# Mixture of experts behind an attention: the last remainders of w2, the token gathers and one part's weight sums in other places

## The chip, the core and the metric

The kernel runs on one core of a Trainium2 chip. The metric is the device time of one execution in microseconds (us); a run is one execution, and the times of several runs are given by their median. The engines are TensorE (PE in the profile; PEld is its weight load), VectorE (DVE), ScalarE (ACT), GpSimd (POOL) and SyncE (SP, which issues transfers). Each engine works through its own queue in order.

## What is computed

An attention over 8 batches and 8 heads (576 rows, 64 columns each, with a decay and a causal mask) gives 4608 tokens of 512 values. A gate picks one of 8 experts for each token, and the expert's two weight matrices are applied to its tokens:

```python
def _moe_ref(x, w_gate, w1, w2):          # x: 4608 x 512, w1: 8 x 512 x 1024, w2: 8 x 1024 x 512
    logits = x @ w_gate
    expert_idx = np.argmax(logits, axis=1)
    ...
    for e in range(E):
        mask = expert_idx == e
        ...
        xe = x[mask]
        h = np.maximum(xe @ w1[e], 0.0)
        ye = h @ w2[e]
        out[mask] = gate_w[mask, None] * ye
    return out.astype(np.float32)
```

## The kernel before

The attention comes first, then the experts one after the other. Expert 0 has a form of its own; the change concerns the experts 1 to 7, which the loop at L1677 runs. Each has room for 640 tokens, in five blocks of 128. Values are kept as two words, a rounded one and a remainder, so that a product is made of three matmuls: rounded by rounded, remainder by rounded, rounded by remainder.

**The ups** (h = relu(x w1)) are 28 steps, k = 0 to 27: four groups (`group`) of seven products each (`product`, L1513, six matmuls a step), a scheme that gets by with seven products of half blocks where eight would be needed. Part i of w1 belongs to group i. A matmul has 320, 288 or 256 columns, by the expert's count of tokens (`by_count`, which branches on PE). Between the products, `after(s)` puts together the four results of a group in banks a, b, g, d: ACT copies p1 = a at s = 0 and p5 = g at s = 2 (L1575, which frees bank g for step 6 of the group); at s = 5 DVE adds b to p1 (L1579), takes it off d (L1580), and POOL adds p1 to p5 (L1581). The rest stands in the next group's first steps: ACT's relu of d and of p5 (L1559, into the rounded h, `hhw`) and of g, DVE's L1590, and DVE's remainders `rest` (L1562, into `hl`). The fourth group's are handed on to the downs as `self.ends`. For group 0 of expert 1 the relu of p5 stands a step later, behind that of g (`late`), and p5 lies in a tile y.

**The downs** (h w2) take a block of 128 tokens each (`down`, m = 0 to 4): 24 matmuls of 512 columns (L1275), eight slices ft of h by three terms, in the order ft = 0, 1, 2, 4, 5, 6, 3, 7. Block 0 (`head`) leaves its last terms to `finish_down`, which comes behind the first six matmuls of block 1. The last block is left out where the expert has no tokens for it, as in expert 5. ACT scales each block (L1303), and POOL scatters it to the output (L1306).

**What runs beside it** is hung on step numbers by hand: `at(ups, (k, f))` puts f behind step k of the ups, `at(dns, ...)` behind a quarter of a block of the downs. `S(...)` is work for this expert, `N(...)` for the next. For w1: `load_s` (SP, L1390), `sums_s` (POOL, four adds L1396 to L1399, tile w1r), `round_s` (ACT, L1411, w1s) and `rest_s` (DVE, or POOL where G is named, L1417); `split_s` is the last two. For w2, in four parts of two slices ft each: `load_v` (SP), `round_v` (ACT, L1456, tile w_0w or w_1w ahead of the remainder) and `rest_v` (DVE, L1449, its remainder); `split_v` is both. For the next expert's tokens: `fetch` (POOL, an indirect gather from x_dram, L1156, tile xg), `put` and `get` (SP, out and back in another layout), `flip` (DVE, L1178).

Of the kernel before, what the change touches and what calls it, by code (L numbers as in the profile page):

```python
# [22 lines left out]
S = 576  # L23
# [15 lines left out]
FT = FF // P  # L39
# [135 lines left out]
def psum(pool):  # L175
    return pool.tile([P, 512], F32, name="ps", tag="ps")
# [13 lines left out]
def attention_all(c, tc, qkT, va, vb, f, wgd, x_dram, batch_done, more_consts, extra):  # L190
# [659 lines left out]
    def run(f):  # L850
        step(f)
        order.pin()

    return run, todo


# [216 lines left out]
class Moe:  # L1073
# [185 lines left out]
    def down(self, e, m, part=(0, FT)):  # L1259

        c, nc = self.c, self.nc
        rows = self.rows_of_h(e, m)
        if part[0] == 0:
            self.py[m] = psum((c.ps_v, c.ps_m)[m % 2])
        py = self.py[m]
        terms = [(ft, *i) for ft in ((0, 1, 2, 4, 5, 6, 3, 7) if e else range(FT))
                 for i in ((0, 0), (0, 1), (1, 0))]
        tail, head = (e > 0 and m == t for t in (NST - 1, 0))
        if head:
            terms.sort(key=lambda t: t in ((6, 0, 1), (7, 0, 1)))  # L1270

        def some(k0, k1):
            for k in range(k0, k1):
                ft, hi_, wi = terms[k]
                c.note(nc.tensor.matmul(  # L1275
                    py, rows(hi_, ft), self.w2p[e, ft][wi],
                    start=k == 0, stop=k == len(terms) - 1, skip_group_check=tail or head,
                ))

        if tail:  # L1280
            some(0, 1)
            few = self.tail
            if e + 1 < E:
                self.begin_up(e + 1)
            else:
                self.tc.mark_branch_hint_location("overflow", engines=[mybir.EngineType.PE])
            with self.tc.If(few > 0):  # L1287
                some(1, len(terms))
        else:
            some(3 * part[0], 3 * part[1] - (2 if head and part[1] == FT else 0))  # L1290
        if part[1] < FT:
            return
        if head:
            self.finish_down = lambda: (some(len(terms) - 2, len(terms)), self.down_out(e, m, py, tail))
        else:
            self.down_out(e, m, py, tail)

# [326 lines left out]
    def run(self, run, tasks):  # L1624
        c, tc = self.c, self.tc
        T = lambda f, *args: lambda: f(*args)
        fetch = lambda e, m: T(self.fetch, e, m)
        self.s, self.parts, self.slots = {}, {}, 0

        def downs(e, ms, tasks):  # L1630
            k = 0
            for m in ms:
                for q in range(4):
                    if e and m == NST - 1:
                        if q == 0:
                            run(lambda: self.down(e, m))
                    else:
                        run(lambda: self.down(e, m, (2 * q, 2 * q + 2)))
                        if e and (m, q) == (1, 0):
                            run(self.finish_down)  # L1640
                    for f in tasks.get(k, []):
                        run(f)
                    k += 1

        with tc.tile_pool(name="moe_w2b", bufs=1, side="right") as w2b:
            self.w2pools.append(w2b)
            self.finish(run, tasks)
            c.note = lambda r: r
            run(lambda: self.begin_h(0, 1))
            S = lambda f, *args: T(f, 1, *args)  # L1650
            self.load_s(1, 0)
            first = {
                0: [S(self.begin_t), fetch(1, 2), fetch(1, 0)],
                2: [S(self.sums_s, 0)], 3: [S(self.turn_t, 3), fetch(1, 1)],
                4: [S(self.turn_t, 4)], 5: [S(self.turn_t, 2)], 6: [S(self.split_s, 0, 0)],
                7: [S(self.turn_t, 0)],
            }
            for ft in range(FT):
                run(lambda: self.up(0, 1, ft))
                for f in first.get(ft, []):  # L1660
                    run(f)
            run(S(self.load_s, 1))
            downs(0, (NA, NA + 1), {
                0: [S(self.turn_t, 1), S(self.split_s, 0, 1), S(self.load_s, 2)],
                1: [S(self.split_t, "T2"), S(self.split_t, "T1")],
                2: [S(self.sums_s, 1), S(self.split_t, "T4"), S(self.split_t, "T3")],
                4: [S(self.split_s, 1, 0), S(self.sums_s, 2)],
                5: [S(self.split_s, 1, 1), S(self.load_s, 3)],
            })
        self.w2st.close()  # L1670
        with tc.tile_pool(name="moe_h", bufs=1) as hp, tc.tile_pool(name="moe_u", bufs=1) as up_, \
                tc.tile_pool(name="moe_r", bufs=2) as self.wr:
            self.up_ = up_
            hl = hp.tile([P, FT * CAP], F32R, name="hl")
            h = [t.rearrange("p (f s) -> p f s", s=CAP) for t in (c.words["hh"], hl)]
            G = self.nc.gpsimd
            for e in range(1, E):  # L1677
                self.h[e] = h
                if e == 1:
                    run(lambda: self.begin_up(e))  # L1680
                S = lambda f, *args: T(f, e, *args)
                N = lambda f, *args: T(f, e + 1, *args)
                ups, dns = {}, {}

                def at(d, *items):
                    for k, f in items:
                        d.setdefault(k, []).append(f)

                late = 9 if e == 1 else 1
                at(ups, (0, S(self.load_v, 0)), (0, S(self.load_v, 1)),  # L1690
                   (4, S(self.round_s, 2, 1)), (6, S(self.rest_s, 2, 1, G)),
                   (late, S(self.load_v, 2)), (late, S(self.load_v, 3)),
                   (9 if e > 1 else 8, S(self.split_s, 3, 0)), (11, S(self.round_s, 3, 1)),
                   (13, S(self.rest_s, 3, 1, G)))
                for i, k in enumerate((15, 22, 16) if e == 1 else (10, 23, 16)):
                    at(ups, (k, S(self.split_v, i)))
                at(ups, (23 if e == 1 else 24, S(self.round_v, 3)))
                if e == 1:
                    at(ups, (0, S(self.sums_s, 3)), (2, S(self.split_s, 2, 0)))
                else:  # L1700
                    at(ups, (8, self.scatter))
                if e + 1 < E:
                    at(ups, (9, N(self.load_s, 0)), (16, N(self.load_s, 1)),
                       (6, fetch(e + 1, 3)), (6, fetch(e + 1, 4)), (13, fetch(e + 1, 2)),
                       (15, fetch(e + 1, 0)), (19, fetch(e + 1, 1)), (20, N(self.sums_s, 0)),
                       (27, N(self.sums_s, 1)))
                    for m, i, k in ((3, 12, 16), (4, 13, 17), (2, 18, 22), (0, 21, 26), (1, 25, 27)):
                        at(ups, (i, N(self.put, m)), (k, N(self.get, m)))
                    at(dns, (0, N(self.begin_t)), (1, N(self.round_s, 0, 0)),
                       (1, N(self.round_s, 0, 1)), (2, N(self.flip, 3)), (2, N(self.flip, 4)),  # L1710
                       (2, N(self.turn_t, 3)), (2, N(self.turn_t, 4)),
                       (2, N(self.rest_s, 0, 0, G)), (2, N(self.rest_s, 0, 1, G)),
                       (6, N(self.flip, 2)), (6, N(self.flip, 0)), (6, N(self.turn_t, 2)),
                       (7, N(self.turn_t, 0)), (7, N(self.load_s, 2)),
                       (7, N(self.split_s, 1, 0)), (8, N(self.round_s, 1, 1)),
                       (8, N(self.rest_s, 1, 1, G)), (8, N(self.flip, 1)),
                       (10, N(self.turn_t, 1)), (11, N(self.load_s, 3)),
                       (12, N(self.split_t, "T2")), (12, N(self.split_t, "T1")),
                       (12, N(self.sums_s, 2)), (14, N(self.split_t, "T4")),
                       (14, N(self.split_t, "T3")), (15, N(self.split_s, 2, 0)),  # L1720
                       (15, N(self.sums_s, 3)))
                else:
                    at(ups, (27, lambda: tc.keep_in_program_order(G.drain())))
                self.ends = [lambda: None] * 3
                self.sevens(e, run, ups)
                dns.setdefault(0, [])[:0] = [*self.ends, T(self.rest_v, 3)]
                downs(e, range(NST), dns)


# [224 lines left out]
```

## Time and profile before

| | |
|---|---|
| median of 3 runs | 727.88 us (727.53 to 728.06) |
| the profiled execution's own time | 727.32 us |
| its span | 725.5 us |
| granted clock of PE | 0.994 |
| busy share of the span: PE, DVE, ACT, POOL | 99%, 77%, 69%, 79% |
| matmuls | 6321 |

Matmuls overlap, and the ends that the trace gives for them are modelled. So a pause of PE is read from the distance between the starts of two matmuls, against the distance that they have where nothing is in the way. A number in square brackets behind a row is idle time of the engine ahead of it, with the instruction that ended it; where PE's records overlap, the number there is smaller than the pause between starts.

### The profile page before, as it was taken

Reading aid. Unit: us, or ns where it says so; the run is one execution under the profiler, and the core shown is the slowest. Engines: PE = TensorE matmul, PEld = TensorE weight load, DVE = VectorE, ACT = ScalarE, POOL = GpSimd, SP = SyncE. Lnnn points to the kernel's source line nnn. Section 1 sums busy time; section 2 is a strip of 40 time slices with the busy share of each in tenths; the row PEclk is TensorE's granted clock in tenths of the full one; section 3 lists DMA queues with packets and bytes.
Section 4 is the critical chain, followed back from the end, with each engine's and each line's share of the span. In section 5 each row is a group of like instructions: output and inputs, shape, how many; then the busy total and the mean of one; then the engine's idle time right before and its main releaser. Section 6 shows DMA issues by size and latency. Waiting matters only on the chain. (4 is left out here: it accounts for less than half of the span.)

```text
span 725.5 us, 18440 instructions
## 1 busy us (share of the span) xinstructions
PE 715.7 (99%) x6321; PEld 617.2 (85%) x6321; DVE 555.9 (77%) x1608; ACT 497.9 (69%) x1319; POOL 573.7 (79%) x702
## 2 busy tenths in 40 slices
PE   9999999999999999999999999999999999999997
PEld 4788888888888888798999898898898888988985
DVE  6668888888888888861879959779589599897730
ACT  6999999999999999562646555566465566655631
POOL 6999989898898898965589779778788797997511
PEclk9999999999999999999999999999999999999999
DMA  6775787766776767334349476386475574673300
GB/s 199 196 193 163 195 215 194 205 197 204 207 205 191 222 187 233 118 117 125 114 150 269 132 231 206 109 249 196 144 208 171 198 214 147 215 208 101 141 30 35
DMA packets 98724, 127.59 MB, mean 176 GB/s; under 512 B 10287, under 2 KB 56367, under 8 KB 98608
## 3 DMA queue, kind: packets, MB, share of 16 engines
q1 hardware_dynamic: 91568, 106.12, 50.3%
q0 software_dynamic: 6400, 19.93, 8.6%
q8 instruction: 71, 1.16, 0.7%
q14 instruction: 45, 0.37, 0.2%
q10 hardware_dynamic: 640, 0.01, 0.0%
HBM read 99.12 MB, written 27.93 MB: 175 GB/s over the span
## 5 line engine op out<-in xcount | busy, mean ns | idle before, releaser
L422 ACT ACTIVATE sc<-sc,nmx 128x512 f32<-128x512 f32 (+3 forms) x256 | 142.4, 558 | 5.3 <-DVE nmx L379 4.2
L1513 PE MATMUL ps<-X_0w,w1s 128*128 128x320 f32 (+2 forms) x504 | 107.0, 303 | 0.7 <-ACT u L1575 0.4
L1275 PE MATMUL ps<-w_0w,hl 128*128 128x512 f32 x272 | 107.3, 395 | 0.0
L1275 PE MATMUL ps<-w_0w,hhw 128*128 128x512 f32 x273 | 106.4, 390 | 0.6 <-ACT hhw L1559 0.6
L1275 PE MATMUL ps<-w_1w,hhw 128*128 128x512 f32 x272 | 105.5, 392 | 0.0
L1306 POOL DMA_INDIRECT out<-y,si_fast x40 | 48.1, 1202 | 59.5 <-ACT y L1303 27.9
L467 ACT COPY aT<-ps 128x512 f32<-128x512 f32 (+1 forms) x224 | 93.4, 507 | 1.8 <-PE ps L455 0.5
L330 POOL TENSOR_TENSOR hl<-raw,hl 128x640 fp32r<-128x640 f32 (+1 forms) x60 | 89.5, 1492 | 5.0
L526 PE MATMUL ps<-aT,va_t 128*64 128x256 f32 (+3 forms) x896 | 91.0, 354 | 0.0
L1513 PEld LDWEIGHTS ps<-X_0w,w1s 128*128 128x128 f32 x504 | 82.3, 188 | 1.2 <-ACT u L1575 0.7
L526 PEld LDWEIGHTS ps<-aT,va_t 128*64 128x64 f32 x896 | 56.6, 137 | 29.0 <-issue 5.3
L403 PE MATMUL ps<-hl 64*128 64x512 f32 (+1 forms) x720 | 80.7, 340 | 0.0
L1513 PE MATMUL ps<-X_1w,w1s 128*128 128x320 f32 (+2 forms) x252 | 75.9, 301 | 0.0
L1303 ACT ACTIVATE y<-ps,g_fast 128x512 f32<-128x512 f32 x40 | 28.0, 699 | 59.5 <-PE ps L1275 51.4
L379 DVE CUSTOM_DVE_ANT_0 sc<-ps,bias 128x128 f32<-128x128 f32 (+1 forms) x128 | 59.8, 486 | 9.3 <-PE ps L403 4.6
L1417 POOL TENSOR_TENSOR w1s<-w1r,w1s 128x768 fp32r<-128x768 f32 (+1 forms) x32 | 62.8, 1968 | 0.1
L1275 PEld LDWEIGHTS ps<-w_0w,hhw 128*128 128x128 f32 x273 | 51.3, 188 | 12.4 <-ACT hhw L1559 1.4
L1275 PEld LDWEIGHTS ps<-w_1w,hhw 128*128 128x128 f32 x272 | 51.1, 188 | 11.5
L1275 PEld LDWEIGHTS ps<-w_0w,hl 128*128 128x128 f32 x272 | 51.1, 188 | 11.1 <-DVE hl L1562 0.6
L379 DVE CUSTOM_DVE_ANT_1 sc<-ps,bias 128x256 f32<-128x256 f32 (+1 forms) x128 | 57.7, 487 | 3.0 <-POOL gT L709 1.7
L1513 PE MATMUL ps<-xa,w1s 128*128 128x320 f32 (+2 forms) x336 | 56.0, 302 | 0.3 <-PEq L1287 0.3
L403 PEld LDWEIGHTS ps<-hl 64*128 64x128 f32 x720 | 52.6, 185 | 3.3
(251 smaller groups left out, 1895.4 us busy)
## 6 DMA issues: line engine op xcount, KB each, us to landing
bias<-ud SPq DMA_DIRECT2D x30, 576.0 KB, 5.8
w1r<-in_w SPq DMA_DIRECT2D x112, 128.0 KB, 2.6
w<-in_w SPq DMA_DIRECT2D x28, 512.0 KB, 5.7
raw<-in_qkT SPq DMA_DIRECT2D x64, 160.0 KB, 3.5
raw<-in_qkT SPq DMA_DIRECT2D x64, 144.0 KB, 3.4
va_t<-in_va SPq DMA_DIRECT2D x32, 256.0 KB, 5.8
x_dram<-row SPq DMA_DIRECT2D x32, 256.0 KB, 2.4
xs<-xg SPq DMA_DIRECT2D x30, 256.0 KB, 3.9
```

Source lines behind the costliest of these rows:

```text
L330: return eng.tensor_tensor(hl[:, 1], raws[n][:, r : r + w], hl[:, 0].bitcast(F32), ALU.subtract)
L379: red_last[:] = [V.tensor_tensor_reduce(dst, src, in1, -0.125, init, ALU.add, ALU.min, nms[n][:, col : col + 1]).ins]
L403: note(nc.tensor.matmul(pb[j][:, o : o + w], q[js], k[js], start=(i == 0), stop=(i == len(terms) - 1),))
L422: A.activation(x, x, AF.Exp, bias=nms[n][:, 5 * j + t : 5 * j + t + 1], scale=-1.0, accum_out=ssums[b][:, t, 2 * p + j : 2 * p + j + 1])
L467: copy_on = {"a": lambda o, i: A.copy(o, i), "v": lambda o, i: V.tensor_copy(o, i)}
L526: note(nc.tensor.matmul(pv[j * HD : (j + 1) * HD, q0 - qa : qb - qa], l, r, start=(blk == 0), stop=(blk == nb - 1),))
L1275: c.note(nc.tensor.matmul(py, rows(hi_, ft), self.w2p[e, ft][wi], start=k == 0, stop=k == len(terms) - 1, skip_group_check=tail or head,))
L1303: nc.scalar.activation(y, py, AF.Copy, scale=g[:, s : s + 1])
L1306: nc.gpsimd.indirect_dma_start(out=self.out, out_offset=bass.IndirectOffsetOnAxis(ap=si[:, s : s + 1], axis=0), in_=y, in_offset=None, bou ...
L1417: (eng or self.nc.vector).tensor_tensor(lo, raw, hi.bitcast(F32), ALU.subtract)
L1513: self.nc.tensor.matmul(bank[:, 0:cols], w[:, wi, mat, kt], x[xi][:, kt, 0:cols], start=start and k == 0, stop=k == 5, skip_group_check=True,)
```

## The change

1. **w2.** In block 0 of the downs of the experts 1 to 7, four terms are left to `finish_down` instead of two: those with the remainder of w2's slices 2, 3, 6 and 7, which are the parts 1 and 3. So 20 matmuls come first, then six of block 1, then four. The remainder of part 1 (`rest_v(1)`) moves from step 23 (22 in expert 1) of the ups to the start of the downs, ahead of that of part 3 and behind what is left of the fourth group.
2. **Gathers.** In the experts 2 to 6 the gathers for the next expert stand behind the steps 1, 1, 8, 8 and 13 instead of 6, 6, 13, 15 and 19; puts and gets go with them, and the load of the next expert's part 1 of w1 goes from step 16 to 20.
3. **Expert 1's sums.** `sums_s(3)` goes from step 0 to step 5, where it stands behind `after(5)` of group 0, and the rounding and remainder of its first half from step 8 to 10.

No engine gets more or fewer instructions.

```diff
         if head:
-            terms.sort(key=lambda t: t in ((6, 0, 1), (7, 0, 1)))
+            late = [(ft, 0, 1) for ft in (2, 3, 6, 7)]
+            terms.sort(key=lambda t: t in late)
...
-            some(3 * part[0], 3 * part[1] - (2 if head and part[1] == FT else 0))
+            n = len(terms) - len(late) if head else 3 * FT
+            some(min(3 * part[0], n), min(3 * part[1], n))
...
-            self.finish_down = lambda: (some(len(terms) - 2, len(terms)), self.down_out(e, m, py, tail))
+            self.finish_down = lambda: (some(n, len(terms)), self.down_out(e, m, py, tail))
...
-                   (9 if e > 1 else 8, S(self.split_s, 3, 0)), (11, S(self.round_s, 3, 1)),
+                   (9 if e > 1 else 10, S(self.split_s, 3, 0)), (11, S(self.round_s, 3, 1)),
...
-                for i, k in enumerate((15, 22, 16) if e == 1 else (10, 23, 16)):
+                for i, k in ((0, 15), (2, 16)) if e == 1 else ((0, 10), (2, 16)):
                     at(ups, (k, S(self.split_v, i)))
-                at(ups, (23 if e == 1 else 24, S(self.round_v, 3)))
+                for i, k in ((1, 22), (3, 23)) if e == 1 else ((1, 23), (3, 24)):
+                    at(ups, (k, S(self.round_v, i)))
                 if e == 1:
-                    at(ups, (0, S(self.sums_s, 3)), (2, S(self.split_s, 2, 0)))
+                    at(ups, (2, S(self.split_s, 2, 0)), (5, S(self.sums_s, 3)))
...
-                    at(ups, (9, N(self.load_s, 0)), (16, N(self.load_s, 1)),
-                       (6, fetch(e + 1, 3)), (6, fetch(e + 1, 4)), (13, fetch(e + 1, 2)),
-                       (15, fetch(e + 1, 0)), (19, fetch(e + 1, 1)), (20, N(self.sums_s, 0)),
-                       (27, N(self.sums_s, 1)))
-                    for m, i, k in ((3, 12, 16), (4, 13, 17), (2, 18, 22), (0, 21, 26), (1, 25, 27)):
+                    if e == 1:
+                        gathers = (6, 3), (6, 4), (13, 2), (15, 0), (19, 1)
+                        ways = (3, 12, 16), (4, 13, 17), (2, 18, 22), (0, 21, 26), (1, 25, 27)
+                    else:
+                        gathers = (1, 3), (1, 4), (8, 2), (8, 0), (13, 1)
+                        ways = (3, 11, 15), (4, 12, 16), (2, 17, 21), (0, 19, 23), (1, 26, 27)
...
-                dns.setdefault(0, [])[:0] = [*self.ends, T(self.rest_v, 3)]
+                dns.setdefault(0, [])[:0] = [
+                    *self.ends, T(self.rest_v, 1), T(self.rest_v, 3)]
```

On POOL, the first steps of expert 6 before (as in the experts 2 to 5): the last sum of a part of w1, the add to p5 of group 0 (u_104), a remainder of w1, then two gathers, a scatter, and the add of group 1.

```order
L1399 TENSOR_TENSOR w1r<-w1r 128x256
L1525 UNCONDITIONAL_BRANCH
L1581 TENSOR_TENSOR u_104<-u_96,u_104 128x320
L1417 TENSOR_TENSOR w1s<-w1r,w1s 128x768
L1156 DMA xg<-x_dram,gi_fast 128x512 x2
L1306 DMA out<-y,si_fast 4608x512
```

The same place after (the lines have moved on by two):

```order
L1401 TENSOR_TENSOR w1r<-w1r 128x256
L1156 DMA xg<-x_dram,gi_fast 128x512 x2
L1527 UNCONDITIONAL_BRANCH
L1583 TENSOR_TENSOR u_104<-u_96,u_104 128x320
L1419 TENSOR_TENSOR w1s<-w1r,w1s 128x768
L1308 DMA out<-y,si_fast 4608x512
L1156 DMA xg<-x_dram,gi_fast 128x512 x2
```

The first pair of gathers now stands ahead of the add of group 0, and the second pair ahead of that of group 1.

On DVE, the end of an expert's fourth group before: a remainder of w2 (into w_0_1w, part 1) stands ahead of the add to p1, and that of part 3 (w_1_1w) behind the last `rest`.

```order
L1449 TENSOR_TENSOR w_0_1w<-w_0_1_94,w_0_0w 128x1024
L1579 TENSOR_TENSOR u_13567<-ps,u_13567 128x320
L1580 TENSOR_TENSOR pr<-u_13567,pr 128x320
L1562 SCALAR_TENSOR_TENSOR hl<-ps,hhw 128x320
L1590 TENSOR_TENSOR ps<-ps,u_13708 128x320
L1562 SCALAR_TENSOR_TENSOR hl<-pr,hhw 128x320
L1562 SCALAR_TENSOR_TENSOR hl<-u_13568,hhw 128x320
L1562 SCALAR_TENSOR_TENSOR hl<-ps,hhw 128x320
L1449 TENSOR_TENSOR w_1_1w<-w_1_1_102,w_1_0w 128x1024
```

The same place after:

```order
L1581 TENSOR_TENSOR u_13567<-ps,u_13567 128x320
L1582 TENSOR_TENSOR pr<-u_13567,pr 128x320
L1564 SCALAR_TENSOR_TENSOR hl<-ps,hhw 128x320
L1592 TENSOR_TENSOR ps<-ps,u_13708 128x320
L1564 SCALAR_TENSOR_TENSOR hl<-pr,hhw 128x320
L1564 SCALAR_TENSOR_TENSOR hl<-u_13568,hhw 128x320
L1564 SCALAR_TENSOR_TENSOR hl<-ps,hhw 128x320
L1451 TENSOR_TENSOR w_0_1w<-w_0_1_94,w_0_0w 128x1024
L1451 TENSOR_TENSOR w_1_1w<-w_1_1_102,w_1_0w 128x1024
```

Both remainders are now a pair behind the group's last `rest`.

On POOL, the start of expert 1 before: the four sums of part 3, then the add of group 0 (into a tile y).

```order
L1306 DMA out<-y,si_fast 4608x512
L1396 TENSOR_TENSOR w1r<-w1r 128x256
L1397 TENSOR_TENSOR w1r<-w1r 128x256
L1398 TENSOR_TENSOR w1r<-w1r 128x256
L1399 TENSOR_TENSOR w1r<-w1r 128x256
L1525 UNCONDITIONAL_BRANCH
L1581 TENSOR_TENSOR y<-u_96,y 128x320
```

The same place after:

```order
L1308 DMA out<-y,si_fast 4608x512
L1527 UNCONDITIONAL_BRANCH
L1583 TENSOR_TENSOR y<-u_96,y 128x320
L1398 TENSOR_TENSOR w1r<-w1r 128x256
L1399 TENSOR_TENSOR w1r<-w1r 128x256
L1400 TENSOR_TENSOR w1r<-w1r 128x256
L1401 TENSOR_TENSOR w1r<-w1r 128x256
```

The sums have gone from ahead of the add to behind it.

## Rows read from the trace of the kernel before

**Rows 1.** Timeline, PE, expert 1: start, length, instruction, count [idle before].

```profile
376.52 0.46 PE L1513 MATMUL ps<-X_0w,w1s 128*128 128x320 f32 x2
376.81 0.31 PE L1513 MATMUL ps<-X_1w,w1s 128*128 128x320 f32 x1
377.56 0.56 PE L1513 MATMUL ps<-X_0w,w1s 128*128 128x320 f32 x2 [0.44 <-ACT u L1575]
377.96 0.31 PE L1513 MATMUL ps<-X_1w,w1s 128*128 128x320 f32 x1
...
383.83 0.46 PE L1513 MATMUL ps<-X_0w,w1s 128*128 128x320 f32 x2
```

**Rows 2.** Timeline, DVE, POOL and ACT, expert 1, groups 0 and 2.

```profile
371.00 0.49 DVE L1579 TENSOR_TENSOR u<-ps,u 128x320 f32<-128x320 f32 x1
...
374.87 0.87 POOL L1581 TENSOR_TENSOR y<-u,y 128x320 f32<-128x320 f32 x1
...
382.85 0.44 ACT L1575 COPY u<-ps 128x320 f32<-128x320 f32 x1
```

**Rows 3.** Timeline, PE and DVE, first product and last L1449, experts 1, 2.

```profile
390.87 0.40 PE L1275 MATMUL ps<-w_0w,hhw 128*128 128x512 f32 x1
...
394.99 1.36 DVE L1449 TENSOR_TENSOR w_1w<-w,w_0w 128x1024 fp32r<-128x1024 f32 x1
...
443.01 0.40 PE L1275 MATMUL ps<-w_0w,hhw 128*128 128x512 f32 x1
...
446.12 1.36 DVE L1449 TENSOR_TENSOR w_1w<-w,w_0w 128x1024 fp32r<-128x1024 f32 x1
```

**Rows 4.** Timeline, PE, first blocks of the downs of experts 3 and 5.

```profile
496.66 0.40 PE L1275 MATMUL ps<-w_0w,hl 128*128 128x512 f32 x1
...
497.92 0.40 PE L1275 MATMUL ps<-w_0w,hhw 128*128 128x512 f32 x1
...
597.52 0.39 PE L1275 MATMUL ps<-w_0w,hhw 128*128 128x512 f32 x1
597.75 0.40 PE L1275 MATMUL ps<-w_0w,hl 128*128 128x512 f32 x1
598.79 0.50 PE L1275 MATMUL ps<-w_0w,hhw 128*128 128x512 f32 x1 [0.64 <-ACT hhw L1559]
...
599.73 0.40 PE L1275 MATMUL ps<-w_0w,hhw 128*128 128x512 f32 x1
```

**Rows 5.** Timeline, POOL and DVE, end of expert 3's fourth group.

```profile
490.03 0.96 POOL L1156 DMA_INDIRECT xg<-x_dram,gi_fast  x1 [0.16 <-issue]
...
492.13 1.71 POOL L1397 TENSOR_TENSOR w1r<-w1r 128x256 f32<-128x256 f32 x1
493.80 0.74 POOL L1398 TENSOR_TENSOR w1r<-w1r 128x256 f32<-128x256 f32 x1
...
495.19 0.88 POOL L1581 TENSOR_TENSOR u<-u,u 128x320 f32<-128x320 f32 x1
...
492.01 1.23 DVE L1449 TENSOR_TENSOR w_1w<-w,w_0w 128x1024 fp32r<-128x1024 f32 x1
```

**Rows 6.** Timeline, POOL, group 0 of expert 2, then of expert 6.

```profile
424.49 0.88 POOL L1581 TENSOR_TENSOR u<-u,u 128x320 f32<-128x320 f32 x1 [2.80 <-DVE u L1579]
...
427.34 1.24 POOL L1156 DMA_INDIRECT xg<-x_dram,gi_fast  x1 [0.16 <-issue]
428.88 1.96 POOL L1156 DMA_INDIRECT xg<-x_dram,gi_fast  x1 [0.30 <-issue]
...
625.78 0.88 POOL L1581 TENSOR_TENSOR u<-u,u 128x320 f32<-128x320 f32 x1
```

**Rows 7.** Timeline, DVE and PE, expert 6, groups 0 to 2.

```profile
627.23 1.60 DVE L1562 SCALAR_TENSOR_TENSOR hl<-u,hhw 128x320 fp32r<-128x320 f32 x1 [0.34 <-ACT hhw L1559]
...
633.53 0.48 DVE L1572 TENSOR_TENSOR u<-ps,u 128x320 f32<-128x320 f32 x1
...
634.68 0.45 PE L1513 MATMUL ps<-X_0w,w1s 128*128 128x320 f32 x2
```

More of the change, by code (lines that the diff above doesn't have):

```diff
@@ L1702, in run @@
                 if e + 1 < E:
-                    at(ups, (9, N(self.load_s, 0)), (16, N(self.load_s, 1)),
-                       (6, fetch(e + 1, 3)), (6, fetch(e + 1, 4)), (13, fetch(e + 1, 2)),
-                       (15, fetch(e + 1, 0)), (19, fetch(e + 1, 1)), (20, N(self.sums_s, 0)),
-                       (27, N(self.sums_s, 1)))
-                    for m, i, k in ((3, 12, 16), (4, 13, 17), (2, 18, 22), (0, 21, 26), (1, 25, 27)):
+                    if e == 1:
[4 more added lines that the diff above has]
+                        ways = (3, 11, 15), (4, 12, 16), (2, 17, 21), (0, 19, 23), (1, 26, 27)
+                    at(ups, (9, N(self.load_s, 0)), (16 if e == 1 else 20, N(self.load_s, 1)),
+                       (20, N(self.sums_s, 0)), (27, N(self.sums_s, 1)),
+                       *((k, fetch(e + 1, m)) for k, m in gathers))
+                    for m, i, k in ways:
                         at(ups, (i, N(self.put, m)), (k, N(self.get, m)))
```

## The prediction

> **What bounds the kernel now.** I read the page first, then each engine's timeline around the experts 1 to 7. TensorE (PE) never rests for long: its work sets the time, and the change leaves that work as it is, for every engine issues as many instructions as before. So the time moves only where PE stands still, and I read that as the distance from start to start in PE's timeline, since ends are modelled. A product of 320 columns follows the last after 0.147 us (two between 376.52 and 376.81), one of 512 columns after 0.229 (597.52 to 597.75) [rows 1, 4]. Against that pitch three places stand out that the change touches. In expert 1, PE stands at step 13: 376.81 to 377.56 is 0.75 for one product of 0.147, and 377.56 to 377.96 is 0.40 for two; 0.60 and 0.11, together **0.71** us, named as a wait for the ACT copy of L1575 [rows 1]. At the start of expert 5's down, 597.75 to 599.73 holds four products, 0.92, and takes 1.98: **1.06**, behind the relu of L1559 [rows 4]. Expert 3 has the same stall in small: 496.66 to 497.92, 1.26 for four, **0.34** [rows 4]. More than 2.11 us the change can't give back.
>
> Next I asked what these waits wait for. All three hang on the add of L1581 on POOL, which the ACT relu of p5 reads; ACT is in order, so the copy of the same expert (step 13) or the relu of g (down) stands behind that relu. At expert 1 the operand p1 is ready at 371.49, yet POOL starts the add at 374.87, since the four sums of part 3 stand ahead of it [rows 2]. At expert 3's group end POOL does a gather (490.03), four sums and only then the add at 495.19; the sum at 492.13 took 1.71 where the one at 493.80 took 0.74 [rows 5].
>
> **Part by part: expert 1's sums behind the add.** The add can start at 371.49 rather than 374.87, 3.4 earlier. Nothing else is late at step 13: the wait is 0.6, and the relu and the copy need POOL alone. **-0.71**. At step 20, PE now comes at 383.83-0.71 = 383.12, and the copy that it needs ends at 382.85+0.44 = 383.29 [rows 1, 2]: **+0.2** (0 to 0.4, since the copy may come earlier with the rest, or wait longer for the hand-over). The sums themselves have until step 8, now 10, for the rounding on ACT; the change delays that with them, so nobody waits.
>
> **The w2 remainder.** One DVE subtraction (L1449) of each expert goes from steps 22/23 to behind the group's last rest, in a pair with the other. Ahead of the group's end this frees DVE: at expert 3 the L1449 at 492.01 for 1.23 stood ahead of the p1 add, and beside it POOL's sum took 0.97 longer [rows 5]. With the gather gone from there too (0.16+0.96 = 1.12 with its gap), POOL reaches the add up to 2.1 earlier. The stalls need 0.34 and 1.06, so both go: **-0.34, -1.06**. Against it, block 0 now does 20 products at first, not 22, so it wants the relu of g one product (0.23) earlier; the 2.1 covers that as well.
>
> A page of the Trainium skill bears on this: by "SBUF — State Buffer", section "Who interferes with whom", a DVE instruction with two SBUF inputs contends with a GpSimd instruction that reads SBUF, over a shared port pair that is an exclusive lock. The trace agrees on the POOL side: 1.71 against 0.74 beside that L1449 [rows 5]. By this rule the 0.97 comes back at the group's end, as taken above, but the pair moved behind the end stands beside the sums of the next expert's part 1, and would lose there what it gained; that is the third rival below.
>
> What the pair costs behind the end: the four late products come as number 27 to 30, so the remainder of part 1 is due 26 pitches after the first product and that of part 3 after 27, at +6.17 us (the latter was due at 28, +6.4). In expert 1 the down starts at 390.87, the last L1449 ends at 394.99+1.36 = 396.35, +5.48. One more in front of it, 1.23 to 1.36 long (I take 1.28), gives +6.76: **+0.6** (0 to 0.6; POOL's gain before the end, up to 0.97, would take it away, but PE gains 0.5 of its own on POOL and DVE there, so I keep it). Expert 2: start 443.01, end 446.12+1.36 = 447.48, +4.47; one more is +5.75, covered by 0.4 [rows 3]. In the experts 3, 5 and 6 the end comes later, but there POOL gains the 2.1 first. I put **+0.2** on all of them (0 to 1.5, third rival).
>
> **The gathers.** For experts 2 to 6, five gathers move to steps 1, 1, 8, 8, 13. The first two now stand on POOL ahead of the add of group 0. Their price: a lone gather took 0.96 with 0.16 of gap [rows 5], the second one's gap is 0.30 [rows 6], so 0.16+0.96+0.30+0.96 = 2.4; from above, expert 2's own pair took 0.16+1.24+0.30+1.96 = 3.66 [rows 6]. I take 2.4, since the long ones stood beside a DVE subtraction. In expert 2 POOL is idle for 2.80 ahead of that add [rows 6], and the experts 3 to 5 have more than that; so the pair costs nothing there, and up to 0.9 if it is long. In expert 6 there is no idle time: POOL runs from the sums straight into the add at 625.78 [rows 6]. So the add comes 2.4 later, and the relu of p5 and the rest of L1562 at 627.23 with it; from there DVE goes without a break up to the add of L1572 at 633.53, which ends at 634.01, and PE reads its result at 634.68 [rows 7]. The margin is 0.67, of which a hand-over of 0.05 is needed: 2.4-0.62 = **+1.8** (0 to 3.0, the latter with the long pair). Part of it shows already at step 13; the sum counts it once. The wait is not given back: POOL does as much between this add and the next as before, in another order.
>
> The puts and gets on SP go with the gathers, and a w1 load goes from step 16 to 20. Its sums stand at step 27, seven steps of six products, 6.2 us, behind; I cost it at nothing. It would cost what the load is late, if it were.
>
> **Sum.** -0.71+0.2-0.34-1.06+0.6+0.2+1.8 = +0.69. The profiled execution took 727.32 (span 725.5), so 728.0; the median of the three runs is 727.88, 0.56 above it. Forecast **728.6** as a median.
>
> **The rivals.** *Expert 6 absorbs its gathers.* What POOL has ahead of that add hangs on weight loads and on work from expert 5's down, where PE now comes an us earlier; if the sums move forward by 2 us, the 1.8 is gone: 726.8, and 726.2 where expert 1's 0.6 is gone too. For it: the add is bound by POOL alone, and POOL leaves expert 5's group end 2.1 earlier. Against it: POOL is continuous there over five sums and more, and each has its own input. 0.20, half of it under 726.4.
>
> *The pair behind the group's end is blocked* (the slower side). POOL does the sums of part 1 in the same 3 us; if one of the pair loses 0.97, expert 1 has +0.97 more, and the experts 2 and 4 end at 5.75+0.97 = 6.72 against 6.17, 0.55 each: 2.1 in all, 730.7. It decides from about 0.7 on, that is when it holds in expert 1 or in two others. For it: 1.71 against 0.74 [rows 5]. Against it: the L1449 there took 1.36 beside sums already [rows 3], only 0.13 over the 1.23 of the other. 0.13.
>
> *The gathers are long in expert 6 as in expert 2.* 3.66 rather than 2.4: 728.6+1.2 = 729.8. For it: expert 2's rows; against it: at expert 6's start other DVE work stands beside them. 0.09.
>
> *The change doesn't do what it says at the group ends.* POOL's add is late in experts 3 and 5 for the sums alone, and the 1.4 stays: 730.0. Against it: 2.1 of gain for 1.06. 0.08.
>
> **How the numbers follow.** The forecast has 0.50, with its own range 727.6 to 729.4 (the bounds of the small terms, and a part of the long pair). A measurement of this kernel tells 0.2%, 1.46 us, from no change: faster is under 726.4, slower over 729.3. Faster 0.10, from half of the first rival. Slower 0.05 of the forecast's edge and the other three rivals, 0.35. Within: 0.45+0.10 = 0.55. The range 726.7 to 730.4 leaves out the lower part of the first rival and the upper part of the second, under 0.2 together.
>
> **What would show it.** In expert 1: no gap in PE's row at step 13, and the add of POOL under 372; a gap of 0.2 at step 20 and one of about 0.6 ahead of the late products. In experts 3 and 5: no wait of PE near the fourth us of the down, POOL's add some 2 us earlier against the down's start. In expert 6: two gathers in one row with the sums, and gaps of PE at steps 13 and 19 of some 0.9 each. I am wrong in the largest term if PE shows none there, and wrong on the pair if the late products wait in more experts than the first.

## The result: 0.8% slower

The changed kernel takes 733.28 us (median of 6 runs, 732.19 to 735.57), the kernel before in the same series 727.92. The ratio is 1.0081 with a 95% interval of 1.0064 to 1.0098: by the medians some 5.4 us more, where 0.7 more had been forecast and a range up to 730.4.

The profiled execution took 732.82, its span is 731.0 at a granted clock of 0.992 (before 725.5 at 0.994). The page of after, the engines:

```profile
PE 718.2 (98%) x6321; PEld 618.2 (85%) x6321; DVE 571.6 (78%) x1608; ACT 497.0 (68%) x1319; POOL 569.9 (78%) x702
```

The instructions are as many as before. DVE is busy for 571.6 us, 15.7 more than before with the same work, and 11.5 of them lie in the subtractions for w1 (L1417 before, L1419 after). That is the first hint. The 5.5 us that the span grew by are best split by stages, from the first product of a stage to the first of the next in PE's timeline (us; e1 is expert 1, the last column from expert 1's first product to the last matmul of the last down):

| kernel | ups e1 | downs e1 | downs e3 | ups e5 | downs e5 | ups e6 | downs e6 | first to last |
|---|---|---|---|---|---|---|---|---|
| before | 25.36 | 27.50 | 27.85 | 21.09 | 23.80 | 24.75 | 27.50 | 354.32 |
| after | 25.53 | 29.24 | 27.53 | 22.28 | 22.70 | 27.02 | 28.33 | 359.31 |

So 4.99 of it lies in the experts 1 to 7. The other 0.48 lies ahead of expert 1, in work that the change leaves alone: its first product came anywhere between 363.3 and 369.0 us in the twelve profiled executions of this study. Each kernel is therefore compared from there on as well, beside the ratio of its runs. The stages not in the table differ by 0.13 at most. Each row of stages is one execution: expert 1's ups took anywhere from 24.65 to 25.36 in the six kernels, here and below, that leave them alone, so up to 0.7 in that column, and in the last, can be this spread.

Where PE waited in after, the largest of the waits that start in these stages, by the view of waits (what waited, for whom, us in total, times, longest):

```profile
PE ps L1515 <- DVE u L1574: 1.9, 3, 1.1
PE ps L1515 <- ACT u L1577: 1.4, 2, 0.9
...
PE ps L1276 <- issue: 1.0, 2, 0.5
PE ps L1276 <- DVE w_1w L1451: 0.4, 1, 0.4
```

The first two lie in the ups of the experts 5 and 6 and in expert 1, the last is the wait of expert 1's late products. The third is new and names no engine: PE stands still once in the last block of expert 1's downs and once in that of expert 6, for 0.63 and 0.68 over the pitch. Timeline of PE and ACT at the first of these places before, then at both after:

```profile
409.01 0.72 ACT L1303 ACTIVATE y<-ps,g_fast 128x512 f32<-128x512 f32 x1
...
412.88 0.39 PE L1275 MATMUL ps<-w_0w,hhw 128*128 128x512 f32 x1
413.11 0.39 PE L1275 MATMUL ps<-w_1w,hhw 128*128 128x512 f32 x1
```

```profile
413.07 0.72 ACT L1305 ACTIVATE y<-ps,g_fast 128x512 f32<-128x512 f32 x1
...
414.49 0.39 PE L1276 MATMUL ps<-w_0w,hhw 128*128 128x512 f32 x1
415.35 0.50 PE L1276 MATMUL ps<-w_1w,hhw 128*128 128x512 f32 x1 [0.47 <-issue]
...
667.87 0.71 ACT L1305 ACTIVATE y<-ps,g_fast 128x512 f32<-128x512 f32 x1
...
669.24 0.39 PE L1276 MATMUL ps<-w_0w,hhw 128*128 128x512 f32 x1
670.15 0.50 PE L1276 MATMUL ps<-w_1w,hhw 128*128 128x512 f32 x1 [0.52 <-issue]
```

The first product of the last block is on time, the second late; between them stands the branch that skips a last block without tokens (its own rows are in the last section). The ACT row is the scaling of block 2, which shares its bank with block 4, the last. It ended 0.70 and 0.66 us ahead of that first product; before, it ended 3.16 us ahead in expert 1 and 3.62 in expert 6.

What made that scaling late is read in the same stage, here of expert 4. First the kernel before, DVE and POOL:

```profile
559.57 1.21 DVE L1417 TENSOR_TENSOR w1s<-w1r,w1s 128x1024 fp32r<-128x1024 f32 x1
...
559.63 2.03 POOL L1306 DMA_INDIRECT out<-y,si_fast  x1 [3.02 <-ACT w1s L1411]
561.66 1.88 POOL L1417 TENSOR_TENSOR w1s<-w1r,w1s 128x768 fp32r<-128x768 f32 x1
```

And after, DVE, POOL and ACT:

```profile
562.59 3.33 DVE L1419 TENSOR_TENSOR w1s<-w1r,w1s 128x1024 fp32r<-128x1024 f32 x1
565.84 1.10 DVE L1178 STREAM_TRANSPOSE ps<-xg 128x512 f32<-128x512 f32 x1
...
561.95 1.00 POOL L1308 DMA_INDIRECT out<-y,si_fast  x1 [3.01 <-ACT w1s L1413]
562.95 1.88 POOL L1419 TENSOR_TENSOR w1s<-w1r,w1s 128x768 fp32r<-128x768 f32 x1
...
567.56 0.71 ACT L1305 ACTIVATE y<-ps,g_fast 128x512 f32<-128x512 f32 x1
568.55 1.00 POOL L1308 DMA_INDIRECT out<-y,si_fast  x1 [3.72 <-ACT y L1305]
```

In the kernel before, DVE's subtraction for the next expert's w1 starts 0.06 us ahead of POOL's scatter; it takes 1.21, and the scatter 2.03 instead of 1.00. In after, DVE comes to the same subtraction 0.64 behind the scatter. Now the scatter takes 1.00, POOL's own remainder follows at once, and DVE's subtraction takes 3.33: it ends 1.1 after POOL's remainder does. The late DVE comes from the pair of w2 remainders, ahead of it in the queue. Behind the subtraction stand the transpose of block 1 of the next expert's tokens, ACT's copies of it, behind these on ACT the scaling of block 2, and behind that POOL's scatter (idle for 3.72) with the sums of w1. The subtraction took 3.28 to 3.53 in the experts 1, 2, 4 and 6 of after, and 1.21 in the experts 3 and 5.

### The profile page after: what moved, and what is told of

It reads as the page before. It is cut to its first block, busy times and chain, and to the rows that moved or that the text cites. A ratio compares the mean times of both kernels' runs of the same rounds, so it can differ in the third digit from the quotient of the medians.

```text
span 731.0 us, 18435 instructions
## 1 busy us (share of the span) xinstructions
PE 718.2 (98%) x6321; PEld 618.2 (85%) x6321; DVE 571.6 (78%) x1608; ACT 497.0 (68%) x1319; POOL 569.9 (78%) x702
## 5 line engine op out<-in xcount | busy, mean ns | idle before, releaser
L1276 PE MATMUL ps<-w_1w,hhw 128*128 128x512 f32 x272 | 103.8, 394 | 1.4 <-issue 1.0
L1308 POOL DMA_INDIRECT out<-y,si_fast x40 | 46.4, 1161 | 68.8 <-ACT y L1305 42.2
L1419 POOL TENSOR_TENSOR w1s<-w1r,w1s 128x768 fp32r<-128x768 f32 (+1 forms) x32 | 62.5, 1961 | 0.1
```

The lines of the kernel that those rows point to most:

```text
L1276: c.note(nc.tensor.matmul(py, rows(hi_, ft), self.w2p[e, ft][wi], start=k == 0, stop=k == len(terms) - 1, skip_group_check=tail or head,))
L1308: nc.gpsimd.indirect_dma_start(out=self.out, out_offset=bass.IndirectOffsetOnAxis(ap=si[:, s : s + 1], axis=0), in_=y, in_offset=None, bou ...
L1419: (eng or self.nc.vector).tensor_tensor(lo, raw, hi.bitcast(F32), ALU.subtract)
```

## The experiments

"After" is the changed kernel; each row of the table is one kernel, the ratio is to the kernel before in the same series.

| kernel | ups e1 | downs e1 | downs e3 | ups e5 | downs e5 | ups e6 | downs e6 | first to last | ratio (95% interval) |
|---|---|---|---|---|---|---|---|---|---|
| w2 part alone | 25.44 | 29.05 | 28.89 | 21.08 | 24.62 | 26.38 | 28.03 | 360.10 | 1.0074 (1.0046 to 1.0101) |
| gathers alone | 24.70 | 27.53 | 27.51 | 21.00 | 22.73 | 26.26 | 27.50 | 353.69 | 1.0000 (0.9981 to 1.0019) |
| sums alone | 25.51 | 27.73 | 27.86 | 21.07 | 23.78 | 24.74 | 27.50 | 354.65 | 1.0021 (1.0005 to 1.0036) |
| after, transpose first | 25.51 | 28.05 | 27.53 | 21.01 | 22.73 | 25.06 | 27.51 | 353.89 | 1.0006 (0.9987 to 1.0025) |
| after, turning late | 25.52 | 27.99 | 27.53 | 21.01 | 22.85 | 25.62 | 27.51 | 354.52 | 1.0002 (0.9983 to 1.0021) |
| before, a transpose twice | 24.77 | 28.57 | 28.82 | 21.08 | 24.61 | 26.33 | 28.15 | 358.78 | 1.0070 (1.0048 to 1.0092) |
| before, transpose first | 24.93 | 27.51 | 27.88 | 21.07 | 23.83 | 24.74 | 27.50 | 353.93 | 0.9995 (0.9980 to 1.0010) |
| gathers, transpose first | 25.03 | 27.51 | 27.50 | 21.02 | 22.72 | 25.12 | 27.50 | 352.87 | 0.9976 (0.9955 to 0.9997) |
| the same, gathers for e2 to e5 | 24.65 | 27.50 | 27.51 | 21.02 | 22.72 | 24.74 | 27.50 | 352.10 | 0.9962 (0.9944 to 0.9980) |
| the same, sums at step 6 | 25.39 | 27.72 | 27.50 | 21.01 | 22.70 | 24.73 | 27.50 | 353.02 | 0.9966 (0.9948 to 0.9984) |

**The three parts apart.** The first three kernels have one part of the change each.

> The kernel before with the w2 part of the change alone (four late terms, both remainders as a pair behind the fourth group); gathers and expert 1's sums as before. Theory A: the pair makes VectorE late for the next expert's work in the downs, so that its subtraction L1417 there (1.2 us before) starts behind POOL's scatter and remainder instead of ahead of them, takes 3.3 to 3.5 us in some of the experts 1, 2, 4, 6, and by way of ACT delays the last block: gaps of PE of 0.7 in the last block of experts 1 and 6, a wait of 0.5 to 0.9 for the late products of expert 1; the stalls of experts 3 (0.34) and 5 (1.06) go. The late sums are absorbed by POOL's 3 us of idle time at the next expert's start, since no gathers stand there: no 1.2 in expert 5's ups. Sum +0.2 to +1.2 us. Theory B (the early gathers are at the root of all, the pair costs only expert 1's 0.6): -0.8 us.

> The kernel before with the early gathers alone. Theory A: expert 6's ups gain 1.8 to 2.3 us of waits, the ends of experts 3 and 5 lose up to 1.1 of their stalls (the gather stands no longer ahead of the sums), L1417 in the downs keeps its 1.2 us, no gap in a last block and none of 1.2 in expert 5's ups: +0.7 to +1.5 us. Theory B (gathers at the root): the gaps of the last blocks and of expert 5's ups are here too, +3 to +4 us.

> The kernel before with expert 1's sums behind the add alone. Both theories: the wait at step 13 of expert 1 (0.71) goes; the trace of the changed kernel shows 0.78 at step 20 instead, as VectorE's L1417 of part 2 meets POOL's (2.65 us for 1.21) and POOL comes to group 1's add 0.5 late. So 0 to +0.2 us if that belongs to the sums; -0.5 if it does not.

The w2 part alone costs as much as the whole change: 1.0074, and 5.8 us in the trace. Theory B, for which it would have gained 0.8, is refuted. Theory A had the kind right and the size far too small (+0.2 to +1.2), since all six subtractions were caught, not four, those of experts 3 and 5 with them. Expert 3's downs went from 27.85 to 28.89. DVE, ACT and PE there, and PE in expert 6's ups:

```profile
510.03 3.40 DVE L1419 TENSOR_TENSOR w1s<-w1r,w1s 128x1024 fp32r<-128x1024 f32 x1
...
515.05 0.71 ACT L1305 ACTIVATE y<-ps,g_fast 128x512 f32<-128x512 f32 x1
...
516.39 0.39 PE L1276 MATMUL ps<-w_0w,hhw 128*128 128x512 f32 x1
517.38 0.50 PE L1276 MATMUL ps<-w_1w,hhw 128*128 128x512 f32 x1 [0.60 <-issue]
...
624.27 0.57 PE L1515 MATMUL ps<-X_0w,w1s 128*128 128x320 f32 x2 [0.77 <-ACT y L1305]
```

Expert 6's ups lose their 1.63 at other steps than in after: 0.93 at step 3, where PE waits for a late ACT scaling of expert 5, and 0.50 at step 5, but none over 0.2 at the steps 13 and 19.

The gathers alone are neutral, under the +0.7 to +1.5 of theory A, and their trace has both signs in it: expert 6's ups +1.51, but the stalls of the experts 3 and 5 are gone without the w2 part (-0.34 and -1.07). The sums alone cost 0.05 to 0.36% in the runs and 0.33 us in the trace, with 0.15 more in expert 1's ups and 0.23 in its downs: step 13 no longer waits, step 20 does.

**Two neighbours exchanged.** If it is the meeting of DVE and POOL that costs, then only what stands behind the subtraction need be taken from there:

```diff
-                       (7, N(self.split_s, 1, 0)), (8, N(self.round_s, 1, 1)),
-                       (8, N(self.rest_s, 1, 1, G)), (8, N(self.flip, 1)),
+                       (7, N(self.round_s, 1, 0)), (8, N(self.round_s, 1, 1)),
+                       (8, N(self.rest_s, 1, 1, G)), (8, N(self.flip, 1)), (8, N(self.rest_s, 1, 0)),
```

> The changed kernel with two neighbours on VectorE exchanged in the downs: the transpose of block 1 of the next expert's tokens (L1178) ahead of the subtraction L1419 of part 1. Theory A: the transpose and with it ACT's copies and the scaling of block 2 no longer wait for POOL, so the gaps in the last blocks of experts 1 and 6 (0.74, 0.78) go, the sums of the next expert come some 2 us earlier and the 1.2 in expert 5's ups goes: 2 to 3 us under the changed kernel, that is +2.4 to +3.4 over before. Theory C (those gaps are code that PE has to wait for): they stay, +5.

```profile
561.58 1.10 DVE L1178 STREAM_TRANSPOSE ps<-xg 128x512 f32<-128x512 f32 x1
562.57 2.33 DVE L1419 TENSOR_TENSOR w1s<-w1r,w1s 128x1024 fp32r<-128x1024 f32 x1
...
561.93 1.88 POOL L1419 TENSOR_TENSOR w1s<-w1r,w1s 128x768 fp32r<-128x768 f32 x1
...
563.44 0.69 ACT L1305 ACTIVATE y<-ps,g_fast 128x512 f32<-128x512 f32 x1
```

These are expert 4's rows: the subtraction is still blocked (2.33), the scaling comes at 16.8 us of the downs instead of 19.9, and no wait of PE in these stages is for the subtraction itself. The changed kernel loses its 5.4 us by this exchange (1.0006 to before), more than the 2 to 3 that I expected: expert 6's ups fell from 27.02 to 25.06 too, since the sums ahead of its add came earlier. The gaps in the last blocks went, though the code is as long as before, so theory C falls with it.

**The scaling alone.** Here the turning of block 1, ACT's copies and DVE's work on them, goes one place back, so that ACT's scaling of block 2 stands ahead of it:

```diff
-                       (10, N(self.turn_t, 1)), (11, N(self.load_s, 3)),
+                       (11, N(self.turn_t, 1)), (11, N(self.load_s, 3)),
```

> The changed kernel with only the turning of block 1 (turn_t, ACT and VectorE) moved one place, from the quarter block 10 of the downs to 11, so that ACT's scaling of block 2 stands ahead of it and no longer behind the late transpose. VectorE still meets POOL. Theory A: PE's gaps in the last blocks (0.74 in expert 1, 0.78 in expert 6) come from the scaling of block 2, which frees the bank that the last block starts in; they go, while the 1.2 of expert 5's ups and the 2.3 of expert 6's stay: 1.0 to 1.8 us under the changed kernel. Theory C (PE waits for its code there): both gaps stay, no gain.

DVE was still blocked in five of the six downs (3.29 to 3.64), and the transpose late. The gaps in the last blocks went, as expected. What I had not expected is that the waits of the ups of experts 5 and 6 shrank with them (22.28 to 21.01, 27.02 to 25.62). By the ratios the gain is 5.7 us, where 1.0 to 1.8 had been expected. So it is the scaling of block 2 through which nearly all of it goes: POOL's third scatter waits for it, and the sums of the next expert stand behind this scatter. What stays is the wait of expert 1's late products and 0.9 us in expert 6's ups. One instruction on ACT, in the wrong place in the order, held the bank of the last block and POOL's queue.

**The delay by itself.** To see whether the w2 part is needed for it at all, the kernel before got one idempotent transpose twice:

```diff
-        self.nc.vector.transpose(
+        for _ in range(2 if m == 3 else 1):
+            self.nc.vector.transpose(
```

> The kernel before with one transpose of the downs (block 3 of the next expert's tokens, L1178, 1.1 us) done twice over, so that VectorE comes 1.0 us later to its subtraction of part 1; w2, gathers and sums are untouched. Theory A (VectorE's delay alone, by the meeting with POOL, is the cause): the subtraction starts behind POOL's scatter in all six downs, takes 3 us or more for 1.2, the scaling of block 2 comes 3 us later, with gaps of PE in the last blocks of experts 1, 3 and 6 and waits of 1 us and more in expert 6's ups: +2.5 to +4.5 us. Theory D (the late products or the rounding of w2 are needed for the loss): the 1.0 us is absorbed, 0 to +0.4 us.

DVE, POOL and PE, expert 1:

```profile
404.23 3.05 DVE L1418 TENSOR_TENSOR w1s<-w1r,w1s 128x1024 fp32r<-128x1024 f32 x1
...
403.30 1.00 POOL L1307 DMA_INDIRECT out<-y,si_fast  x1 [3.18 <-DMA out<-y,si_fast]
404.30 1.89 POOL L1418 TENSOR_TENSOR w1s<-w1r,w1s 128x768 fp32r<-128x768 f32 x1
...
410.04 0.39 PE L1276 MATMUL ps<-w_0w,hhw 128*128 128x512 f32 x1
411.20 0.50 PE L1276 MATMUL ps<-w_1w,hhw 128*128 128x512 f32 x1 [0.77 <-issue]
```

One microsecond more on DVE in each of the six downs, with w2, gathers and sums untouched, costs 4.5 us in the trace and 1.0070 in the runs, in the same stages as the w2 part, at the upper end of the 2.5 to 4.5 expected. All six subtractions took 2.88 to 3.05. Theory D falls.

> The kernel before with the exchange of after_flip_first alone (transpose of block 1 ahead of the subtraction of part 1). Theory A: VectorE is ahead of POOL in every expert of the kernel before, so there is no loss to take away; the scaling of block 2 comes 1.2 us earlier, where it ends no wait: 0, at most -0.3 us.

The counterpart: with the exchange in the kernel before, five of the six subtractions now meet POOL and take 2.93 to 3.19, and the time stays (0.9995). Here the block costs nothing that the runs resolve; it is what stands behind the blocked instruction.

**A version under both.** The rest of the change, with the exchange, and without the w2 part and, in the first two, without the sums:

> The kernel before with the early gathers and with the transpose of block 1 ahead of the subtraction of part 1 on VectorE; the w2 part and expert 1's sums as before. Theory A: the stalls of experts 3 and 5 are gone as with the gathers alone (-0.34, -1.07), the sums of the next expert come earlier, so that expert 6's ups lose 0.3 to 1.0 instead of 1.5; no waits in the downs of expert 1: -0.2 to -1.0 us against before.

> As gathers_flip, with the gathers of expert 6 at their places of before. Theory A: expert 6's ups are as before (24.75 us from first product to first), the rest as in gathers_flip: -1.2 to -1.5 us. If the waits of expert 6 had another cause than the two gathers ahead of the add, they stay.

> As gathers25_flip, with expert 1's sums of part 3 one step further than in the change, at step 6 behind POOL's remainder of part 2 (L1417). If expert 1's wait at step 20 comes from VectorE meeting POOL's L1417 after the sums, it shrinks from 0.78 to under 0.3 and the one at step 13 is gone: 0.4 to 0.7 us under gathers25_flip where that has its wait of 0.71 at step 13. If POOL's sum of work up to the second add sets step 20, 0.8 stays there.

The first came out at 0.9976 and lost 0.37 in expert 6's ups, within the 0.3 to 1.0 expected. The second has the lowest ratio of this study, though the intervals of the other two overlap with its own: 0.9962, some 2.8 us under the kernel before (2.3 by the medians) and, by the two ratios, 8.6 under the changed one. In its trace 1.08 come from expert 5's downs, 0.34 from those of expert 3, and 0.71 from a step 13 of expert 1 that did not wait in that execution. With expert 6's gathers back at their places its ups take 24.74 again; 0.38 was their price with the exchange (25.12), 1.51 without. Moving the sums of expert 1 one step further left 0.53 of the wait at step 20, not under 0.3, so that wait is POOL's sum of work up to the second add more than the meeting on the way. The expected gain of 0.4 to 0.7 did not come; it had been tied to a wait at step 13 in the second kernel, which its trace does not have.

## The prediction, point by point

**The step that failed** is what the w2 pair costs behind the group's end. I followed the pair to the late products and no further, and priced it at 0.6 in expert 1 and 0.2 elsewhere. DVE's queue goes on behind it: transposes, subtraction, transposes, with ACT and POOL waiting for them. My text named nothing that is queued behind the pair. With the w2 part alone the whole loss is there (5.8 us in the trace), and with a delay of DVE alone most of it (4.5). In after it measured +1.74 in expert 1's downs (0.64 at the late products, 0.74 in the last block, 0.29 ahead of both, at the products that wait for the group's last remainder on DVE, L1564) and +0.83 in those of expert 6, +1.19 in expert 5's ups through the late sums, and 0.76 of expert 6's ups (27.02 against 26.26 with the gathers alone): some 4.5 us in all, where the sum had 0.8. The sign that I had named for being wrong on the pair, late products that wait in more experts than the first, did not show in after; the loss lay elsewhere.

For expert 5's ups I had written that the gathers cost nothing, covered by POOL's idle time ahead of the add. That cover was real before [rows 6 for expert 2], 3.28 in expert 5, but the late sums used it up. POOL of before, then POOL and PE of after, expert 5:

```profile
578.21 0.88 POOL L1581 TENSOR_TENSOR u<-u,u 128x320 f32<-128x320 f32 x1 [3.28 <-DVE u L1579]
```

```profile
579.86 0.99 POOL L1156 DMA_INDIRECT xg<-x_dram,gi_fast  x1
581.15 0.96 POOL L1156 DMA_INDIRECT xg<-x_dram,gi_fast  x1 [0.30 <-DVE ps L1582]
582.14 0.88 POOL L1583 TENSOR_TENSOR u<-u,u 128x320 f32<-128x320 f32 x1
...
590.42 0.51 PE L1515 MATMUL ps<-X_0w,w1s 128*128 128x256 f32 x2 [1.08 <-DVE u L1574]
```

The add stands at 6.92 us of the ups instead of 5.25. It takes both parts: with either alone expert 5's ups are 21.0 to 21.1.

**The second rival** (the prediction also calls it the third) had the right rule in the wrong place. I looked for DVE and POOL meeting at the pair itself. There they did meet, for 0.4 on DVE: the pair took 3.04 in expert 1, where I had 2.6. POOL lost more there: two sums beside the pair took 1.72 and 1.73, where one takes 0.74. PE at the late products:

```profile
397.82 0.40 PE L1276 MATMUL ps<-w_1w,hhw 128*128 128x512 f32 x1
398.58 0.96 PE L1276 MATMUL ps<-w_1w,hhw 128*128 128x512 f32 x3 [0.36 <-DVE w_1w L1451]
399.38 0.39 PE L1276 MATMUL ps<-w_0w,hhw 128*128 128x512 f32 x1
```

PE waited 0.53 there and another 0.11 in the three behind it, where I had 0.6 (these rows answer to [rows 3]). The costly meeting is some ten microseconds further on, at 408.16.

The rule of the Trainium skill that the prediction weighed ("SBUF — State Buffer", section "Who interferes with whom") describes that meeting: an exclusive lock between a DVE instruction with two SBUF inputs and a reading GpSimd instruction. The traces agree with it for the subtractions, 1.21 against 3.33 beside POOL's.

**Expert 1's sums** were mis-sized: -0.5 expected for the ups, +0.17 found. The wait at step 13 [rows 1] is gone, but it goes on at step 20 with 0.78 (0.66 and 0.12), where I had 0.2. DVE, POOL and PE of after:

```profile
376.42 2.65 DVE L1419 TENSOR_TENSOR w1s<-w1r,w1s 128x1024 fp32r<-128x1024 f32 x1 [0.44 <-ACT w1s L1413]
...
376.13 1.84 POOL L1419 TENSOR_TENSOR w1s<-w1r,w1s 128x768 fp32r<-128x768 f32 x1
378.13 1.79 POOL L1156 DMA_INDIRECT xg<-x_dram,gi_fast  x1 [0.16 <-issue]
...
384.26 0.56 PE L1515 MATMUL ps<-X_0w,w1s 128*128 128x320 f32 x2 [0.50 <-ACT u L1577]
```

The work on POOL up to the second add is the same, and two blocked instructions came to it. I held the copy of step 20 at its old time, 17.34 us behind expert 1's first product (382.85, [rows 2]); it came 17.80 behind it. Also the 0.71 at step 13 was no fixed price: with the gathers alone, where expert 1 is untouched, that step had no wait. Expert 1's ups took 25.39 to 25.53 in the five kernels with the sums moved, more than in any that leaves those ups alone.

**Expert 6's gathers** were nearly right: 1.8 forecast, 1.51 with the gathers alone; POOL's pair and gaps took 2.26 there (622.14 to 624.40), where I had 2.4. In after it is 2.27, for the add came at 10.74 us of the ups instead of 7.93, 2.8 later: PE had come 1.1 earlier out of expert 5's downs, and POOL's sums only 0.8 earlier. The first rival wanted 2 there; the long pair of gathers, 3.66, was not seen. Timeline of after:

```profile
628.66 0.99 POOL L1156 DMA_INDIRECT xg<-x_dram,gi_fast  x1 [0.15 <-issue]
629.96 0.96 POOL L1156 DMA_INDIRECT xg<-x_dram,gi_fast  x1 [0.30 <-DMA out<-y,si_fast]
630.94 0.88 POOL L1583 TENSOR_TENSOR u<-u,u 128x320 f32<-128x320 f32 x1
...
633.04 0.56 PE L1515 MATMUL ps<-X_0w,w1s 128*128 128x320 f32 x2 [0.86 <-ACT u L1577]
639.20 0.56 PE L1515 MATMUL ps<-X_0w,w1s 128*128 128x320 f32 x2 [0.62 <-DVE u L1574]
```

The waits stand at the two steps that were named, 13 and 19.

**The stalls of experts 3 and 5** [rows 4] went, by 0.32 and 1.10, as forecast (0.34 and 1.06). But the gathers alone do that; the w2 part was not needed for it.

## What to carry to other kernels

When an instruction is moved on an in-order engine, follow everything queued behind it up to the next wait that PE has, not only its own readers: 1 us more on VectorE in each of six experts cost 4.5 us here, at waits that came ten microseconds and more behind it. Where two engines block each other and one starts only 0.06 us ahead of the other, as here, that order is a resource; either put nothing that matters behind the blocked instruction, or expect any shift to turn it round. And the block alone is no loss: exchanging two neighbours, so that the blocked subtraction stood last, brought the changed kernel back to the time before (1.0006).

## What the runs showed of the hardware

POOL's indirect DMA is in this lock too: the scatter took 2.03 where DVE's subtraction had started 0.06 ahead, and 1.00 where it had not. A DVE subtraction that came during the scatter got its turn only behind the next POOL instruction: 3.33 is the rest of the scatter, all of the following remainder, and 1.1 of its own. This is not settled fully. With the gathers alone, two subtractions that started 0.63 and 0.68 behind a scatter still took 1.22, and the POOL remainder behind took 2.55 and 2.61 instead, and two more in kernels with the transpose first, 0.17 and 0.29 behind, took 1.20; what decides between these two outcomes was not tried.

The gap in the last block follows the scaling of block 2 to a few hundredths of a us. Between the last block's first product and its second, PE's queue reads two values from tables (`begin_up`, L1535) and takes the branch (L1288). The trace lists these among the instructions of PE's sequencer, here by source line for expert 1 (count, length in ns, start in us), after and then before:

```profile
L1535 PEldq TENSOR_LOAD <-arms x1: 313/313/313, 413.8 to 413.8; - x1
...
L1288 PEldq COMPARE_BRANCH  x1: 73/73/73, 415.2 to 415.2; - x1
```

```profile
L1287 PEldq COMPARE_BRANCH  x1: 73/73/73, 411.1 to 411.1; - x1
```

In after the first read starts with the scaling's end (413.07 + 0.72 = 413.79), and the branch comes just ahead of the second product at 415.35. Before, the branch was done 1.7 us ahead of even the first product at 412.88. In all eight downs with a gap, of three kernels, the first read started 0.05 us behind the scaling's end and the second product 1.56 to 1.61. In the six downs where the scaling ended 1.34 to 1.54 us ahead of the first product, with the pitch of 0.23 on top, at most 0.1 was left of the gap. So the product that waits for its bank holds back the reads and the branch behind it in PE's queue, though by its own row it starts on time.
